# Plain float32 matmuls in three of the four transform stages of a Fourier mixing and feed-forward kernel

## The chip, the cores and the metric

The kernel runs on one core of a Trainium2 chip, as one launch. The metric is the time on the device in microseconds (us); a smaller time is better. TensorE (PE, with its weight loads shown apart as PEld), VectorE (DVE), ScalarE (ACT), GpSimd (POOL) and the DMA queues of SyncE (SP) and POOL take part.

## The reference, cut to what matters

The input `x` has 4 batches of 3072 rows and 256 columns, all float32. Three layers follow one another; the change touches the first alone, the Fourier mixing.

```python
X = np.fft.rfft(x, axis=1)                      # along the 3072 rows
Xr, Xi = X.real.astype(np.float32), X.imag.astype(np.float32)
Yr = Xr @ w_r - Xi @ w_i + b_r
Yi = Xr @ w_i + Xi @ w_r + b_i
Yr = np.sign(Yr) * np.maximum(np.abs(Yr) - lam, 0.0)      # lam = 0.01, Yi likewise
y = np.fft.irfft(Y, n=3072, axis=1)             # Y = Yr + 1j*Yi
# then: a token-shifted feed-forward layer (256 -> 1024 -> 256, squared relu, sigmoid gate)
# then: a second feed-forward layer (256 -> 2048 -> 256, h * clip(h + 3, 0, 6) / 6)
```

## The kernel before, in words

A transform of 3072 rows is made as 96 x 32 with two matmul stages in each direction. Per batch there are four transform stages and the mixing between them:

- `s1` multiplies a 96 x 96 table `f1` with the rows of `x`. A chunk is 96 partitions x 512 elements; each batch has 16 chunks, two to a step. The result goes through ACT to DRAM (`sc_a`).
- `mid` walks over 12 blocks `j`. It reads a chunk of 128 x 512 from `sc_a`. `s2(j)` multiplies each of the chunk's four 128 x 128 pieces, as the stationary operand, with a table of 192 columns (`tt`). Block 0 has a piece of three tables of 64, 64 and 128 columns, twice, with the extra table `tex`. `mix(j)` is the product with `w_r` and `w_i`, followed by the soft threshold; `ia(j)` is the first inverse stage. The result goes to `sc_b`.
- `ib` is the last inverse stage. A chunk of 96 x 512 from `sc_b` is four stationary pieces of 96 x 128, against the 96 x 96 table `fi`. Two chunks make one step, and a batch has 8 steps. The result goes to `sc_y`, from where the first feed-forward layer (`u_r`, `u_k`, `u_v`) reads it.

Matmuls run in the type F32R, whose operands the kernel rounds to 12 significant bits (`_round12`, line 36, for the tables). For float32 accuracy each operand is divided into a rounded part and the remainder (`split`, lines 152 to 155: ACT writes the high part, DVE the low part), and `three` (line 157) adds three products: high by high, low by high, high by low. The tables come divided from the host. `ib` instead lays the high and the low table side by side as one moving operand of 192 columns, multiplies it with the high and the low data (lines 450 and 451), and adds the two halves of the result afterwards (ACT line 454, DVE line 455).

Chunks are loaded by `load_chunks` (line 266, SP queue, 5 buffers `a`), divided by `split_chunks` (line 277, 4 buffers each of `ah` and `al`) and used by `take`. `fetch` (line 296) divides up to four chunks past those in use and loads four more than that. All transform stages share the chunk list, in program order.

PE, ACT, DVE and POOL run in the order in which the program is written; SP's order is planned. PSUM tiles of two banks come from a ring of three (`ptile`, line 149), shared by the transforms and the first feed-forward layer. `first` (line 481) holds the transforms of batch 0 and part of batch 1, which run before the feed-forward layer starts; the remaining transform steps (`later`) are drawn one by one between the units of the first feed-forward layer. The weights of the feed-forward layers arrive as 64-bit floats and are decoded on ACT and DVE (lines 203 to 219) beside this. The second feed-forward layer (lines 739 to 841) comes last and has no transforms beside it.

Of the kernel before, what the change touches and what calls it, by code (L numbers as in the profile page):

```python
# [9 lines left out]
F32 = mybir.dt.float32  # L10
# [15 lines left out]
LAM = 0.01  # L26

# [20 lines left out]
def _tables():  # L48
# [45 lines left out]
    ext = np.stack(_pair(fwd[0, :, 0, 64:128]), 1)  # L94
    fwd = np.concatenate([fwd[:, :, :, 0:64], fwd[:, :, :, 128:256]], 3)
    tab = np.zeros((NP + 2, 128, 2, 640), np.float32)
    tab[:NP, :, :, 0:384] = np.concatenate(_pair(fwd), 3)
    tab[2:, :, :, 384:640] = np.concatenate(_pair(inv), 3)
    small = np.concatenate([*_pair(f1), *_pair(f1.T)], 1)
# [4 lines left out]
def fourier_mix_ffn_kernel(  # L104
# [133 lines left out]
    with tc.manual_schedule(engines=order):  # L238
# [4 lines left out]
        f1 = cst.tile([N1, 2, N1], F32R, name="f1")  # L243
        pad(cst, 128)
        fi = cst.tile([N1, 2, N1], F32R, name="fi")
# [8 lines left out]
        tex = fp.tile([128, 2, 64], F32R, name="tex")  # L254
# [6 lines left out]
        head = {"load": 0, "split": 0, "use": 0}  # L261
# [4 lines left out]
        def load_chunks(upto):  # L266
            while head["load"] < min(len(chunks), upto) and chunks[head["load"]][1] in ready:
                n = head["load"]
                src, _, p = chunks[n]
                if pad_a:  # L270
                    pad(fp, pad_a.pop())
                a = fp.tile([128, 2, D], F32, tag="a", bufs=5, name="a")
                nc.sync.dma_start(out=a[:p], in_=src)
                live[n] = (a[:p], p)
# [12 lines left out]
        def take(n):  # L287

            u = head["use"]
            load_chunks(u + n)  # L290
            split_chunks(u + n)
            r = [live.pop(u + i) for i in range(n)]
            head["use"] = u + n
            return r

        def fetch():

            split_chunks(head["use"] + 4)
            load_chunks(head["split"] + 4)

        def s1(b, lo, hi):
            for s in range(lo, hi):
                p = ptile("s1")
# [12 lines left out]
                yield  # L316
# [16 lines left out]
        def mid(b):  # L333
# [6 lines left out]
            def s2(j):  # L340
                ((h, l),) = take(1)
                t = tt[b, j]
                p = ptile("s2")
                for g in range(2):
                    for dt in range(2):
                        d = slice(128 * dt, 128 * dt + 128)
                        hl = (h[:, g, d], l[:, g, d])
                        if j or g:
                            c = 512 * g + 192 * dt
# [45 lines left out]
            def ia(j):  # L395
                yh, yl = yy.pop(j)
                t = tt.pop((b, j + 2))[:, :, 384:640]
# [40 lines left out]
        def ib(b, lo, hi):  # L438
            ty = sc_y[b].rearrange("a p n -> p a n")
            r = fi.rearrange("p s n -> p (s n)")  # L440
            for c in CHUNKS[lo:hi]:
                n0 = N1 + 4 * c * N1
                sb = fp.tile([128, 2, 4, N1], F32, tag="ev", bufs=3, name="ysb")
                for q, (h, l) in enumerate(take(2)):
                    p = ptile("ib").rearrange("p (a n f) -> p a n f", a=2, n=2)
                    for et in range(2):
                        e = slice(128 * et, 128 * et + 128)
                        for i in range(2):
                            o = p[:, et, i, 0:192]
                            nc.tensor.matmul(o, h[:, i, e], r, start=True, stop=False)  # L450
                            nc.tensor.matmul(o, l[:, i, e], r, start=False, stop=True)  # L451
                    co = fp.tile([128, 512], F32, tag="co", bufs=2, name="co")
                    co = co[:, 0:384].rearrange("p (a n f) -> p a n f", a=2, n=2)
                    nc.scalar.activation(co, p[:, :, :, 96:192], AF.Copy)
                    nc.vector.tensor_add(sb[:, :, 2 * q : 2 * q + 2], p[:, :, :, 0:96], co)
# [11 lines left out]
        def plan(kind, b, lo=0, hi=0):  # L467
            if kind == "s1":
                v = x[b].rearrange("(p n) d -> p n d", n=N2)
                chunks.extend((v[:, 2 * c : 2 * c + 2], None, N1) for c in range(2 * lo, 2 * hi))  # L470
                return kind, s1(b, lo, hi)
            if kind == "mid":
                v = sc_a[b].rearrange("(j g c) n d -> j (c n) g d", g=2, c=4)
                chunks.extend((v[j], ("a", b), 128) for j in range(NP))
                return kind, mid(b)
            for c in CHUNKS[lo:hi]:
                chunks.extend((sc_b[b][:, n : n + 2], ("b", b), N1) for n in (4 * c, 4 * c + 2))
# [17 lines left out]
        nc.gpsimd.dma_start(out=f1.rearrange("p s n -> p (s n)"), in_=small[:, 0 : 2 * N1])  # L495
        load_chunks(5)
# [356 lines left out]
        split_chunks(4)  # L853
        load_chunks(7)
# [18 lines left out]
        for step, _ in enumerate(stream(first)):  # L873
# [8 lines left out]
            if step == LOAD_FI:  # L882
                nc.gpsimd.dma_start(out=fi.rearrange("p s n -> p (s n)"), in_=small[:, 2 * N1 : 4 * N1])
# [194 lines left out]
```

## Time and profile before

| what | value |
|---|---|
| median of 3 runs | 2042.8 us |
| the three runs | 2042.8, 2043.0, 2040.19 us |
| span of the profiled execution | 2040.3 us |
| PE busy | 1978.7 us (97%) |
| PE weight loads busy | 1837.8 us (90%) |
| DVE busy | 1539.0 us (75%) |
| ACT busy | 1330.0 us (65%) |
| mean granted TensorE clock | 0.982 |

The profile gives one time of the profiled execution, its span from the first to the last instruction: 2040.3 us, 2.5 us under the median of the runs. Times inside the trace count from the span's start. A matmul's end is modelled, so the distance between two starts tells more than a duration does. A weight load overlaps the matmul before it. The granted clock is a share of full speed, with the levels 0.5 (1.2 GHz) and 1 (2.4 GHz). A "wait" is idle time of an engine ahead of an instruction, with what ended it.

### The profile page before, as it was taken

The page shows a single profiled execution, that of the slowest core. Times are in us where ns is not written, and L with a number is a line of the kernel's source. Part 1 is how long each engine was busy: PE and PEld are TensorE (multiplying, and loading weights), DVE is VectorE, ACT ScalarE, POOL GpSimd, SP SyncE. Part 2 cuts the span into 40 slices and gives each one's busy share as a digit, 9 for nine tenths or more (in the row PEclk, how much of TensorE's full clock was granted, in tenths as well). Part 3 has the DMA queues.
Part 4 walks back from the last instruction along what each step waited for, and adds up shares of the span by engine and source line. Part 5 has one row for each costly group of instructions (what it writes and reads, how often), then busy time and mean ns, then how long its engine had stood idle before and what let it go on. Part 6 is the DMA issues. An engine that isn't in the chain of part 4 may idle for free.

```text
span 2040.3 us, 34155 instructions
## 1 busy us (share of the span) xinstructions
PE 1978.7 (97%) x13928; PEld 1837.8 (90%) x13928; DVE 1539.0 (75%) x1929; ACT 1330.0 (65%) x1965; POOL 34.7 (2%) x63
## 2 busy tenths in 40 slices
PE   5879999999999999999999999999999999999998
PEld 3868998899789988877789999999999999999998
DVE  3768667766776687888878787778877787778876
ACT  4567557655765575666647676666666676666665
POOL 0000000000000000000000000000000000000000
PEclk7978999999999999999999999999999999999999
DMA  9776447544653352222110110010100110000100
GB/s 255 229 220 188 123 117 217 184 134 124 209 172 112 93 173 89 83 68 85 54 31 22 32 32 22 22 28 26 32 22 22 32 32 22 22 27 27 32 11 22
DMA packets 106991, 175.88 MB, mean 86 GB/s; under 512 B 12945, under 2 KB 63314, under 8 KB 106834
## 3 DMA queue, kind: packets, MB, share of 16 engines
q1 hardware_dynamic: 96034, 141.76, 22.4%
q0 software_dynamic: 10480, 31.67, 5.8%
q8 instruction: 109, 1.79, 0.4%
q14 instruction: 48, 0.39, 0.1%
q10 hardware_dynamic: 320, 0.26, 0.0%
HBM read 110.35 MB, written 63.31 MB: 85 GB/s over the span
## 4 chain that ended last, share of the span: by engine, by line
PE 80%; DVE 11%; ACT 5%; DMA 3%; issue 2%; SPq 0%; ACTq 0%; DVEq 0%
PE oacc L835 25%; PE rq L835 15%; PE acc L163 9%; PE pk L163 8%; PE cc L835 6%; PE mix L163 6%; PE s L163 4%; PE pr L163 2%; DVE g L585 2%; DVE gl L586 1%; PE ia L163 1%; PE ib L450 1%; PE ib L451 1%; PE pi L163 1%; DVE xf L543 1%
## 5 line engine op out<-in xcount | busy, mean ns | idle before, releaser
L835 PE MATMUL oacc<-wo_hi,gl 128*128 128x256 f32 x1536 | 425.6, 277 | 1.1 <-DVE gl L776 1.1
L835 PE MATMUL oacc<-wo_hi,gh 128*128 128x256 f32 x1536 | 426.2, 277 | 0.0
L835 PE MATMUL oacc<-wo_lo,gh 128*128 128x256 f32 x1536 | 424.7, 276 | 0.0
L835 PEld LDWEIGHTS oacc<-wo_hi,gl 128*128 128x128 f32 x1536 | 289.2, 188 | 1.8 <-DVE gl L776 1.5
L835 PEld LDWEIGHTS oacc<-wo_hi,gh 128*128 128x128 f32 x1536 | 289.1, 188 | 0.2
L835 PEld LDWEIGHTS oacc<-wo_lo,gh 128*128 128x128 f32 x1536 | 288.6, 188 | 0.0
L767 DVE SCALAR_TENSOR_TENSOR g<-g,c 128x1024 f32<-128x1024 f32 x184 | 225.5, 1226 | 53.0 <-ACT g L763 52.5
L776 DVE TENSOR_TENSOR gl<-g,gh 128x1024 fp32r<-128x1024 f32 x184 | 225.3, 1224 | 49.8 <-ACT gh L773 46.9
L763 ACT ACTIVATE g<-c,half 128x1024 f32<-128x1024 f32 x184 | 211.8, 1151 | 5.1 <-DVE c L758 4.9
L753 ACT ACTIVATE s<-rq 128x256 f32<-128x256 f32 x184 | 70.5, 383 | 220.9 <-PE rq L835 220.9
L835 PE MATMUL rq<-th,sw 128*128 128x256 f32 x1104 | 212.0, 281 | 0.1
L757 DVE TENSOR_TENSOR c<-rq,s 128x512 f32<-128x512 f32 x184 | 126.8, 689 | 97.2 <-ACT s L753 97.1
L773 ACT ACTIVATE gh<-g 128x1024 fp32r<-128x1024 f32 x184 | 193.7, 1053 | 1.6 <-DVE g L767 1.6
L585 DVE TENSOR_TENSOR g<-g 128x1024 f32<-128x1024 f32 x96 | 117.4, 1223 | 79.6 <-ACT gh L584 79.4
L835 PEld LDWEIGHTS rq<-th,sw 128*128 128x128 f32 x1104 | 168.8, 189 | 0.3 <-ACT s L742 0.3
L163 PE MATMUL acc<-gl,wv_hi 128*128 128x512 f32 x384 | 151.8, 395 | 7.1 <-DVE gl L586 6.9
L835 PE MATMUL rq<-tl,sw 128*128 128x256 f32 x552 | 155.0, 281 | 0.6 <-DVE tl L716 0.6
L163 PE MATMUL pk<-kh,wk_hi 128*128 128x512 f32 x384 | 150.6, 392 | 0.8 <-ACT g L580 0.8
L163 PE MATMUL acc<-gh,wv_hi 128*128 128x512 f32 x384 | 151.3, 394 | 0.0
L163 PE MATMUL acc<-gh,wv_lo 128*128 128x512 f32 x384 | 150.2, 391 | 0.0
L163 PE MATMUL pk<-kl,wk_hi 128*128 128x512 f32 x384 | 149.7, 390 | 0.0
L163 PE MATMUL pk<-kh,wk_lo 128*128 128x512 f32 x384 | 149.5, 389 | 0.0
(152 smaller groups left out, 4955.7 us busy)
## 6 DMA issues: line engine op xcount, KB each, us to landing
tt<-in_tab_dram POOLq DMA_DIRECT2D x40, 640.0 KB, 4.8
yt<-sc_y SPq DMA_DIRECT2D x23, 608.0 KB, 3.9
a<-in_x_dram SPq DMA_DIRECT2D x64, 192.0 KB, 3.7
sc_a<-s1sb SPq DMA_DIRECT2D x32, 384.0 KB, 3.9
a<-sc_a SPq DMA_DIRECT2D x48, 256.0 KB, 3.4
sc_b<-iasb SPq DMA_DIRECT2D x48, 256.0 KB, 4.3
a<-sc_b SPq DMA_DIRECT2D x64, 192.0 KB, 3.1
sc_y<-ysb SPq DMA_DIRECT2D x32, 384.0 KB, 2.8
```

Of the source, the lines that this page charges most:

```text
L163: nc.tensor.matmul(o, a, c, start=first and i == 0, stop=last and i == n - 1, **kw)
L450: nc.tensor.matmul(o, h[:, i, e], r, start=True, stop=False)
L451: nc.tensor.matmul(o, l[:, i, e], r, start=False, stop=True)
L543: nc.vector.scalar_tensor_tensor(o, y[:, a, 0 : hi - lo], mus[:, w, a : a + 1], o, op0=ALU.mult, op1=ALU.add)
L585: nc.vector.tensor_mul(g, g, g)
L753: nc.scalar.activation(s[:, 3], q, AF.Copy)
L757: nc.vector.tensor_add(c[:, 1::2], two(rq), s[:, 0:2])
L763: nc.scalar.activation(g, c, AF.Relu, bias=half, scale=1.0 / 6.0)
L767: nc.vector.scalar_tensor_tensor(g, g, 1.0, tmp["c"], op0=ALU.min, op1=ALU.mult)
L773: nc.scalar.activation(h, tmp["g"], AF.Copy)
L776: nc.vector.tensor_sub(hg[i, j][1], tmp["g"], hg[i, j][0].bitcast(F32))
L835: return lambda: nc.tensor.matmul(o, lhs, rhs, start=start, stop=stop, skip_group_check=True)
```

## The change

`s1`, `s2` and `ib` take the loaded chunk as it is, with undivided float32 tables, one plain float32 matmul in place of three (or, in `ib`, two) F32R matmuls. The chunks' division (`split_chunks`, the tiles `ah` and `al`) goes. `ib` puts both chunks of a step into one PSUM tile, one bank each, and copies the result out by ACT for one half of the columns and by DVE for the other, with no sum. Loads run up to `AHEAD` = 8 chunks past those in use, with 10 buffers; the first call loads 8 chunks instead of 5. The tables shrink: 448 columns per block instead of 640, and half of `f1`, `fi` and `tex`. `mix` and `ia` stay as they are.

```diff
-        f1 = cst.tile([N1, 2, N1], F32R, name="f1")
+        f1 = cst.tile([N1, N1], F32, name="f1")
-        fi = cst.tile([N1, 2, N1], F32R, name="fi")
+        fi = cst.tile([N1, N1], F32, name="fi")
-        tex = fp.tile([128, 2, 64], F32R, name="tex")
+        tex = fp.tile([128, 64], F32, name="tex")
@@ load_chunks
-                a = fp.tile([128, 2, D], F32, tag="a", bufs=5, name="a")
+                a = fp.tile([128, 2, D], F32, tag="a", bufs=AHEAD + 2, name="a")
-        def split_chunks(upto):
-            while head["split"] < min(upto, head["load"]):
-                n = head["split"]
-                a, p = live[n]
-                h = fp.tile([128, 2, D], F32R, tag="ah", bufs=4, name="ah")
-                l = fp.tile([128, 2, D], F32R, tag="al", bufs=4, name="al")
-                split(a, h[:p], l[:p])
-                live[n] = (h[:p], l[:p])
-                head["split"] += 1
@@ fetch
-            split_chunks(head["use"] + 4)
-            load_chunks(head["split"] + 4)
+            load_chunks(head["use"] + AHEAD)
@@ s1
-                for i, (h, l) in enumerate(take(2)):
-                    three(p[:N1, 512 * i : 512 * i + 512], [((f1[:, 0], f1[:, 1]), (flat(h), flat(l)))])
+                for i, a in enumerate(take(2)):
+                    nc.tensor.matmul(p[:N1, 512 * i : 512 * i + 512], f1, flat(a), start=True, stop=True)
@@ load_t
-                t = fp.tile([128, 2, 640], F32R, tag="t", bufs=3, name="tt")
-                c = slice(0 if j < NP else 384, 640 if j >= 2 else 384)
+                t = fp.tile([128, 2, 448], F32R, tag="t", bufs=3, name="tt")
+                c = slice(0 if j < NP else 192, 448 if j >= 2 else 192)
@@ s2
-                            three(p[:, c : c + 192], [(hl, (t[:, g, 0:192], t[:, g, 192:384]))])
+                            mm(512 * g + 192 * dt, 192, a[:, g, d], t[:, g, 0:192])
                         else:
-                            three(p[:, c : c + 64], [(hl, (t[:, g, 0:64], t[:, g, 192:256]))])
-                            three(p[:, c + 64 : c + 128], [(hl, (tex[:, 0], tex[:, 1]))])
-                            three(p[:, c + 128 : c + 256], [(hl, (t[:, g, 64:192], t[:, g, 256:384]))])
+                            mm(c, 64, a[:, g, d], t[:, g, 0:64])
+                            mm(c + 64, 64, a[:, g, d], tex)
+                            mm(c + 128, 128, a[:, g, d], t[:, g, 64:192])
@@ ib
-                for q, (h, l) in enumerate(take(2)):
-                    p = ptile("ib").rearrange("p (a n f) -> p a n f", a=2, n=2)
+                p = ptile("ib").rearrange("p (q f) -> p q f", q=2)[:, :, 0 : 4 * N1]
+                p = p.rearrange("p q (a n f) -> p q a n f", a=2, n=2)
+                for q, a in enumerate(take(2)):
                     for et in range(2):
                         for i in range(2):
-                            nc.tensor.matmul(o, h[:, i, e], r, start=True, stop=False)
-                            nc.tensor.matmul(o, l[:, i, e], r, start=False, stop=True)
-                    nc.scalar.activation(co, p[:, :, :, 96:192], AF.Copy)
-                    nc.vector.tensor_add(sb[:, :, 2 * q : 2 * q + 2], p[:, :, :, 0:96], co)
+                            lhs = a[:, i, 128 * et : 128 * et + 128]
+                            nc.tensor.matmul(p[:, q, et, i], lhs, fi, start=True, stop=True)
+                for et in range(2):
+                    o = sb[:, et].rearrange("p (q n) f -> p q (n f)", q=2)
+                    v = p[:, :, et].rearrange("p q n f -> p q (n f)")
+                    if et:
+                        nc.vector.tensor_copy(o, v)
+                    else:
+                        nc.scalar.activation(o, v, AF.Copy)
@@ before the loops
-        load_chunks(5)
+        load_chunks(AHEAD)
```

## Rows read from the trace of the kernel before

**Rows 1.** The page's first part: busy time, share of the span, instructions.

```profile
PE 1978.7 (97%) x13928; PEld 1837.8 (90%) x13928; DVE 1539.0 (75%) x1929; ACT 1330.0 (65%) x1965; POOL 34.7 (2%) x63
```

**Rows 2.** Busy us by stretch: length, PE, PEld, DVE, ACT, POOL, clock, DMA, GB/s.

```profile
0.00:42.00 42.00, 22.08 (x61) 12.07 (x61) 13.25 (x25) 21.71 (x32) 3.37 (x9) 0.85 0.90 251
42.00:131.20 89.20, 73.47 (x529) 70.36 (x530) 67.15 (x107) 53.18 (x88) 8.28 (x14) 0.88 0.73 222
131.20:141.50 10.30, 6.18 (x18) 3.35 (x16) 2.56 (x4) 5.82 (x10) 0.54 (x1) 0.68 0.84 263
141.50:200.40 58.90, 53.90 (x256) 47.30 (x257) 50.16 (x80) 45.84 (x76) 1.07 (x2) 0.74 0.64 198
200.40:816.00 615.60, 612.28 (x3616) 538.64 (x3616) 434.15 (x553) 387.95 (x548) 21.47 (x37) 1.00 0.48 146
...
1071.00:2040.30 969.30, 963.00 (x8296) 962.20 (x8294) 761.47 (x900) 661.61 (x1033) 0.00 (x0) 1.00 0.09 26
```

**Rows 3.** Groups by line and form: busy us, mean ns, idle before, releasers.

```profile
L155 DVE TENSOR_TENSOR al<-a,ah 96x512 fp32r<-96x512 f32 x128 | 82.8, 682 | 45.5 <-ACT ah L154 45.5
L154 ACT ACTIVATE ah<-a 96x512 fp32r<-96x512 f32 x128 | 74.3, 622 | 15.3 <-DMA a<-in_x_dram 9.5 <-DMA a<-sc_b 5.6
L455 DVE TENSOR_TENSOR ysb<-ib,co 128x384 f32<-128x384 f32 x64 | 33.5, 551 | 13.5 <-ACT co L454 13.4
L155 DVE TENSOR_TENSOR al<-a,ah 128x512 fp32r<-128x512 f32 x48 | 31.7, 683 | 0.8 <-ACT ah L154 0.8
```

**Rows 4.** PE's timeline in `s1`, start and duration in us: low, then full clock.

```profile
8.45 1.06 PE L163 MATMUL s<-ah,f 96*96 96x512 f32 x2
...
9.73 1.06 PE L163 MATMUL s<-ah,f 96*96 96x512 f32 x2
...
22.57 0.62 PE L163 MATMUL s<-ah,f 96*96 96x512 f32 x2
...
23.26 0.62 PE L163 MATMUL s<-ah,f 96*96 96x512 f32 x2
```

**Rows 5.** PE's timeline in `s2`: 64 columns at low clock, 192 at full.

```profile
45.51 0.40 PE L163 MATMUL s<-tex,ah 128*128 128x64 f32 x1
45.73 0.40 PE L163 MATMUL s<-tex,al 128*128 128x64 f32 x1
...
62.17 0.39 PE L163 MATMUL s<-tt,ah 128*128 128x192 f32 x2
...
62.50 0.39 PE L163 MATMUL s<-tt,ah 128*128 128x192 f32 x2
```

**Rows 6.** PE's timeline in `ib` at full clock, two pieces' starts.

```profile
378.01 0.28 PE L450 MATMUL ib<-fi,ah 96*128 96x192 f32 x1
...
378.24 0.27 PE L450 MATMUL ib<-fi,ah 96*128 96x192 f32 x1
```

**Rows 7.** PE's waits from 200.4 to 816 us: us in total, times, longest.

```profile
PE ib L450 <- DVE ysb L455: 3.1, 3, 1.8
```

**Rows 8.** PE's waits from 42 to 131.2 us.

```profile
PE mix L163 <- DVE yf L384: 8.7, 5, 2.0
PE s L163 <- ACT ah L154: 8.1, 1, 8.1
PE s L163 <- DVE al L155: 2.7, 1, 2.7
```

**Rows 9.** PE's timeline: two starts after idle time, idle us and releaser.

```profile
16.10 1.17 PE L163 MATMUL s<-ah,f 96*96 96x512 f32 x2 [3.73 <-ACT ah L154]
...
182.97 0.53 PE L450 MATMUL ib<-fi,ah 96*128 96x192 f32 x1 [2.19 <-DVE ysb L455]
```

**Rows 10.** The chain of waits in `mid` of batch 0: start, us, what.

```profile
76.82 4.60 PE mix L163 x24
...
84.31 0.96 DVE Xl L155
...
89.97 4.63 PE mix L163 x24
```

More of the change, by code (lines that the diff above doesn't have):

```diff
@@ L26 @@
 LAM = 0.01
+AHEAD = 8
 CHUNKS = (1, 2, 3, 4, 5, 6, 7, 0)
@@ L93, in _tables @@
     inv = inv.reshape(NP, 2, 128, 128).transpose(0, 2, 1, 3)
-    ext = np.stack(_pair(fwd[0, :, 0, 64:128]), 1)
+    ext = fwd[0, :, 0, 64:128].astype(np.float32)
     fwd = np.concatenate([fwd[:, :, :, 0:64], fwd[:, :, :, 128:256]], 3)
[L96 to L99, printed above, removed]
+    tab = np.zeros((NP + 2, 128, 2, 448), np.float32)
+    tab[:NP, :, :, 0:192] = fwd
+    tab[2:, :, :, 192:448] = np.concatenate(_pair(inv), 3)
+    small = np.concatenate([f1, f1.T], 1).astype(np.float32)
     return [np.ascontiguousarray(a) for a in (tab, ext, small)]
@@ L253, in fourier_mix_ffn_kernel @@
         bias = fp.tile([128, 3, D], F32, name="bias")
-        tex = fp.tile([128, 2, 64], F32R, name="tex")
+        tex = fp.tile([128, 64], F32, name="tex")
         chunks = []
         ready = set()
-        head = {"load": 0, "split": 0, "use": 0}
+        head = {"load": 0, "use": 0}
         live = {}
@@ L268, in load_chunks @@
                 n = head["load"]
-                src, _, p = chunks[n]
+                src, _, p, _ = chunks[n]
                 if pad_a:
                     pad(fp, pad_a.pop())
-                a = fp.tile([128, 2, D], F32, tag="a", bufs=5, name="a")
+                a = fp.tile([128, 2, D], F32, tag="a", bufs=AHEAD + 2, name="a")
                 nc.sync.dma_start(out=a[:p], in_=src)
-                live[n] = (a[:p], p)
+                live[n] = a[:p]
                 head["load"] += 1
-        def split_chunks(upto):
-            while head["split"] < min(upto, head["load"]):
-                n = head["split"]
-                a, p = live[n]
-                h = fp.tile([128, 2, D], F32R, tag="ah", bufs=4, name="ah")
-                l = fp.tile([128, 2, D], F32R, tag="al", bufs=4, name="al")
-                split(a, h[:p], l[:p])
-                live[n] = (h[:p], l[:p])
-                head["split"] += 1
         def take(n):
@@ L290, in take @@
             load_chunks(u + n)
-            split_chunks(u + n)
             r = [live.pop(u + i) for i in range(n)]
@@ L340, in s2 @@
             def s2(j):
-                ((h, l),) = take(1)
-                t = tt[b, j]
+                (a,) = take(1)
+                t = tt[b, j].bitcast(F32)
+                mm = lambda c, w, lhs, rhs: nc.tensor.matmul(p[:, c : c + w], lhs, rhs, start=True, stop=True)
                 p = ptile("s2")
@@ L396, in ia @@
                 yh, yl = yy.pop(j)
-                t = tt.pop((b, j + 2))[:, :, 384:640]
+                t = tt.pop((b, j + 2))[:, :, 192:448]
                 p = ptile("ia")
@@ L439, in ib @@
             ty = sc_y[b].rearrange("a p n -> p a n")
-            r = fi.rearrange("p s n -> p (s n)")
             for c in CHUNKS[lo:hi]:
@@ L443, in ib @@
                 sb = fp.tile([128, 2, 4, N1], F32, tag="ev", bufs=3, name="ysb")
-                for q, (h, l) in enumerate(take(2)):
-                    p = ptile("ib").rearrange("p (a n f) -> p a n f", a=2, n=2)
+                p = ptile("ib").rearrange("p (q f) -> p q f", q=2)[:, :, 0 : 4 * N1]
+                p = p.rearrange("p q (a n f) -> p q a n f", a=2, n=2)
+                for q, a in enumerate(take(2)):
                     for et in range(2):
-                        e = slice(128 * et, 128 * et + 128)
                         for i in range(2):
-                            o = p[:, et, i, 0:192]
-                            nc.tensor.matmul(o, h[:, i, e], r, start=True, stop=False)
-                            nc.tensor.matmul(o, l[:, i, e], r, start=False, stop=True)
-                    co = fp.tile([128, 512], F32, tag="co", bufs=2, name="co")
-                    co = co[:, 0:384].rearrange("p (a n f) -> p a n f", a=2, n=2)
-                    nc.scalar.activation(co, p[:, :, :, 96:192], AF.Copy)
-                    nc.vector.tensor_add(sb[:, :, 2 * q : 2 * q + 2], p[:, :, :, 0:96], co)
+                            lhs = a[:, i, 128 * et : 128 * et + 128]
[7 more added lines that the diff above has]
+                        nc.scalar.activation(o, v, AF.Copy)
                 nc.sync.dma_start(out=ty[:, :, n0 : n0 + 4 * N1], in_=sb.rearrange("p a n f -> p a (n f)"))
@@ L469, in plan @@
                 v = x[b].rearrange("(p n) d -> p n d", n=N2)
-                chunks.extend((v[:, 2 * c : 2 * c + 2], None, N1) for c in range(2 * lo, 2 * hi))
+                chunks.extend((v[:, 2 * c : 2 * c + 2], None, N1, True) for c in range(2 * lo, 2 * hi))
                 return kind, s1(b, lo, hi)
@@ L473, in plan @@
                 v = sc_a[b].rearrange("(j g c) n d -> j (c n) g d", g=2, c=4)
-                chunks.extend((v[j], ("a", b), 128) for j in range(NP))
+                chunks.extend((v[j], ("a", b), 128, False) for j in range(NP))
                 return kind, mid(b)
             for c in CHUNKS[lo:hi]:
-                chunks.extend((sc_b[b][:, n : n + 2], ("b", b), N1) for n in (4 * c, 4 * c + 2))
+                chunks.extend((sc_b[b][:, n : n + 2], ("b", b), N1, False) for n in (4 * c, 4 * c + 2))
             return kind, ib(b, lo, hi)
@@ L493, in fourier_mix_ffn_kernel @@
         wv = Weights(kw_p, w_v, 8, D, "wv")
-        nc.gpsimd.dma_start(out=f1.rearrange("p s n -> p (s n)"), in_=small[:, 0 : 2 * N1])
-        load_chunks(5)
+        nc.gpsimd.dma_start(out=f1, in_=small[:, 0:N1])
+        load_chunks(AHEAD)
         nc.vector.memset(zero, 0.0)
@@ L849, in store @@
                     at += m
-        split_chunks(4)
-        load_chunks(7)
         loads = decoder(wr.jobs + wk.jobs + wv.jobs, stage1)
@@ L882, in fourier_mix_ffn_kernel @@
             if step == LOAD_FI:
-                nc.gpsimd.dma_start(out=fi.rearrange("p s n -> p (s n)"), in_=small[:, 2 * N1 : 4 * N1])
+                nc.gpsimd.dma_start(out=fi, in_=small[:, N1 : 2 * N1])
             if step in DECODE:
```

2 lines of the change are left out of this document (removed).

## The prediction, made before the result was known

> **What bounds the kernel now.** The first view to read is the page's busy line: PE is busy for 97% of the span, DVE for 75%, ACT for 65% [rows 1]. A share of busy time is a mean over unlike stages, so the second view is the table by stretch [rows 2]. From 200.4 to 816 us PE is busy for 612.3 of 615.6 us at the full clock, while DVE is busy for 434 and ACT for 388: there only PE's own time counts, and relief on DVE or ACT is worth little. From 1071 us on there is no transform. The first 200.4 us are another matter: PE is busy for 155.6 of them, and the granted clock has means of 0.85, 0.88, 0.68 and 0.74 in the four stretches. Of its levels, 0.5 and 1 (1.2 and 2.4 GHz), a mean of 0.74 says that the low one held for about half of the time. Here PE waits for others, and what it waits for decides. The third view, the starts on PE's timeline, gives the price of a product [rows 4 to 6]; the fourth, PE's waits and the chain, says who comes last [rows 7 to 10].
>
> **Price of a product.** An F32R product of 512 columns takes 0.23 us at full clock (three from 22.57 to 23.26) and 0.427 us at low clock (three from 8.45 to 9.73) [rows 4]. One of 192 columns takes 0.111 us [rows 5], more than its 192/512 of 0.23, which is 0.086. At low clock one of 64 columns takes 0.22 us, twice 0.111, though it has a third of the columns [rows 5]. So short products pay a floor of 0.11 us at full clock, which is the load of their 128 stationary columns and not the stream.
>
> The trace shows no plain float32 product. The nearest rows bound it. The kernel rounds each F32R operand to 12 significant bits and divides its data for that reason; a product of undivided operands needs all four products of the halves, where the kernel makes three. I take two passes, one for each half of the stationary operand, in each of which both halves of the moving operand stream: two passes of twice the columns, each with one load beside it. Ends of the price: 4 x 0.2133 us (half of the low-clock 0.427, no time lost between products) and, above, a load that nothing hides (rival B).
>
> - `s1`, 1024 columns a pass: 0.853 to 0.92 (4 x 0.23), taken 0.89, where three products take 0.69 [rows 4]: **+0.20 us a chunk**.
> - `s2`, 384 columns: 0.75 x 0.23 = 0.17 a pass, 0.345 for two, where three take 0.333 (62.17 to 62.50 [rows 5]): **+0.012** a piece; the low end is 0.32.
> - `s2`, block 0: nine products, 9 x 0.111 = 1.0, become six passes of 128, 128 and 256 columns, all near the floor: 0.67, so **-0.33** each.
> - `ib`, 192 columns a pass: the same two loads and columns as now, 0.23 a piece [rows 6]: **0**. If a plain load has a lower floor, 2 x 0.086 = 0.172, so -0.058.
>
> **Where only PE counts.** By the code, 34 `s1` chunks are drawn after the first part, and batches 1 to 3 have 138 ordinary `s2` pieces, 6 of block 0 and 192 of `ib`. That is 34 x 0.20 = 6.8, plus 1.7, minus 2.0, plus 0: **+6.5 us**. The divisions leave DVE and ACT: 82.8 and 31.7 us of `al` on DVE, about as much on ACT [rows 3]. `ib`'s sum on DVE (64 x 0.55 us) becomes 32 copies of the same size, half of it [rows 3]. That shortens the only wait of PE in this stretch, 3.1 us for `ysb` [rows 7]; I take back 2.5. Together **+4.0 us**.
>
> **The first 200 us.** Start: PE idles 3.73 us at 16.10 for a division that waits for its chunk [rows 9]. The new first call issues eight chunks, not five, ahead of the two weight loads, and a buffer is free as soon as PE has read it. But DMA is busy for 0.90 of this stretch [rows 2], and `s1` gets dearer. I take **-3**, ends -5 and +6 (rival C). The depth itself is not new: four divided and four more loaded are eight now.
>
> First blocks of `mid`: PE stops 8.1 us until `ah` is there and then 2.7 us for `al`, which on DVE stands behind two small vector instructions that wait for a transfer [rows 8]. Without a division PE starts when the chunk lands: 0.62 (one `ah` [rows 3]) and 2.7 us earlier. Block 0 at the low clock saves two times three floors of 0.22, 1.3 us. Late next is the low half of the mixing weights, behind `Xl` on DVE. Taken **-4**, ends 0 and -5.
>
> Loop of `mid` of batch 0: the chain runs `mix`, `ia`, `s2`, `Xh`, `Xl`, `yl`, a weight decode, `yf`, and `mix` again: 13.15 us for two blocks (76.82 to 89.97 [rows 10]). No `ah` or `al` is on it, and `s2` costs the same: **0**, although DVE is busy for 67 of 89 us [rows 2]. `mix` waits for `yf` 8.7 us in total [rows 8], and that stays. Ends -4 and +4, with the clock at which `mix` falls.
>
> End of that `mid`: two `al` (1.36 us [rows 3]) stand on DVE ahead of the last `yl`, and dearer `s1` steps lie between on PE. **-1**, ends -2 and +1.
>
> `ib` of batch 0, 141.5 to 200.4 us: DVE is busy for 50.2 of 58.9 us and PE's clock is 0.74 [rows 2]. Both chunks of a step now share one PSUM tile, so a step claims one of the ring's three where it claimed two; its copies start only after the second chunk, about 0.9 us later for the first, and the two run side by side. The wait of 2.19 us at 182.97 [rows 9], behind decode and divisions, should go. After it the `ib` products are 0.21 us apart, low clock, so it costs some 3 us more. Taken **-4**, ends 0 and -14, the latter if the clock stays high throughout: half of the 58.9 us at half speed.
>
> **Sum:** +4.0 - 3 - 4 + 0 - 1 - 4 = **-8 us**. The span of 2040.3 becomes 2032.3; the 2.5 us between span and median are carried over: 2042.8 - 8 = **2035**.
>
> SP's queue: a load waited for the `al` that frees its buffer, with stores queued behind it; with ten buffers the slot it needs belongs to a chunk already used. I cost that at nothing beyond the start. The smaller tables save DMA time, which only the start feels.
>
> **Rivals.** *A, the forecast:* 0.62. For it: `al` on DVE where PE waits, and the prices above.
>
> *B, the loads of plain products are not hidden:* 0.13. Each pass then pays its stream and a load of 0.11 in turn. `s1` is 1.12 (+0.43 x 34 = 15), `s2` 0.57 (+0.24 x 138 = 33), `ib` 0.40 (+0.17 x 192 = 33): +81 in place of +6.5, **2110, slower**. Against it: for F32R the load lies beside the stream [rows 4 to 6]. There are some 760 passes after 200 us, so slower by 0.2% begins at 16 ns more a pass.
>
> *C, the clock stays low in the first 200 us:* 0.15. A chunk of `s1` at low clock takes 1.71, not 1.28. Twenty take 34 us; PE's 22.1 busy us there [rows 2] and some 6 idle us between would hold 28. So +6 in place of -3, and the -4 of `ib` is lost as well: **2048**. It decides once more than about 12 of 20 run at low clock. For it: the clock there is 0.85 already, and waits remain.
>
> *D, one pass is enough:* 0.07. Then the columns double but the loads don't: `s1` 0.46 (-0.23 x 34), `s2` 0.17 (-0.16 x 138), `ib` 0.115 (-0.115 x 192), block 0 about as in A: -54 in place of +6.5, **1974**. Against it: four products of halves don't fit in two streams. The Trainium skill, "Perfetto Trace Analysis", section Engine Utilization, puts the output rate of FP32_LOW_HIGH at half; if that is the whole product and not one pass of it, it is D. No row here shows it.
>
> *E, the relief buys nothing* (transfers set the start, chains elsewhere stay), and gains cancel the +4: 0.03, **2042**.
>
> **How the numbers follow.** A is likeliest: 2035. Its own range, with the ends of the prices and of the first 200 us, is 2019 to 2044. B and D (0.20 together) are left out; C is taken in: 2016 to 2050. About 0.2%, 4 us, is what a measurement can tell from no change. Faster: 0.53 of A, 0.02 of C, all of D: 0.62. Same: 0.06 of A, 0.06 of C, E: 0.15. Slower: 0.03 of A, 0.07 of C, B: 0.23.
>
> **What would show it.** On PE's timeline: `s1` products 0.89 us a chunk, `s2` pieces 0.345, `ib` pieces 0.23; over 0.95, 0.40 and 0.30 speak for B, half of them for D. In the table: the steady stretch about 4 us longer, PE still full, DVE at some 340 us in place of 434. The first `mix` some 7 us earlier; two blocks of the loop still 13 us; the `ysb` waits gone. The forecast is wrong if the loop of `mid` gets shorter, which would mean that its chain was not as read, or if the steady stretch gets shorter.

## The result and the profile after

The kernel after takes 2019.9 us (median of 4 runs, 2019.21 to 2020.22), the kernel before 2042.57 (4 runs, 2040.19 to 2043.0): a ratio of 0.9894 [0.9881, 0.9908], 22.7 us faster. The forecast was 2035, so the direction holds and the size is off by a factor of nearly three (8 us forecast, 22.7 measured). The profiled execution has a span of 2018.1 us; its page answers to [rows 1]:

```profile
PE 1970.9 (98%) x13656; PEld 1812.8 (90%) x13656; DVE 1417.5 (70%) x1721; ACT 1228.0 (61%) x1757; POOL 34.6 (2%) x63
```

PE's busy time fell by 7.8 us, a third of the gain; the rest was idle time. The table by stretch over the same times as [rows 2] (columns as there):

```profile
0.00:42.00 42.00, 27.85 (x66) 13.42 (x66) 2.64 (x10) 14.38 (x15) 4.47 (x11) 0.88 0.93 263
42.00:131.20 89.20, 71.47 (x459) 61.38 (x459) 57.38 (x90) 45.55 (x71) 7.63 (x13) 0.92 0.68 210
...
141.50:200.40 58.90, 58.64 (x334) 52.68 (x333) 39.05 (x53) 37.55 (x51) 1.60 (x3) 0.93 0.59 185
200.40:816.00 615.60, 615.21 (x3412) 530.56 (x3412) 362.68 (x423) 325.88 (x418) 20.94 (x36) 1.00 0.45 134
```

Equal times hold unequal work here, because the kernel after is ahead. So the starts of the same instruction in both traces say where the gain arose (timelines of ACT, DVE and PE; us from the span's start):

| start of | before | after | difference |
|---|---|---|---|
| the eighth copy out of `s1` (batch 0 done) | 29.77 | 24.19 | -5.6 |
| first `yf` of `mid` | 55.89 | 50.79 | -5.1 |
| fourth `yf` | 76.08 | 71.08 | -5.0 |
| last `yf` of batch 0 | 123.83 | 115.23 | -8.6 |
| first `ib` product | 142.13 | 132.00 | -10.1 |
| second sigmoid (`r`) of the feed-forward layer | 205.97 | 186.45 | -19.5 |
| 17th sigmoid (transforms done) | 818.15 | 795.69 | -22.5 |
| end | 2040.32 | 2018.06 | -22.3 |

Start and first blocks gave 5.1 us (forecast 7), the loop of `mid` 3.5 (0), its end 1.5 (1), `ib` of batch 0 9.4 (4), and the steady stretch 2.9, where 4.0 were to be lost.

PE's waits in the first 210 us answer to [rows 8] and [rows 9]. The waits for `ah` and `al` are gone; in the transforms' products loads stand in their place. The largest wait is another: `ia` stands 7.1 us for `yh`, 5.8 of it once, behind the late first `yf` (e8). The loads:

```profile
PE s L332 <- DMA a<-sc_a: 5.7, 1, 5.7
...
PE ib L437 <- DMA a<-sc_b: 3.0, 1, 3.0
PE s L295 <- DMA a<-in_x_dram: 2.5, 4, 1.1
```

PE's timeline after shows the prices (start, duration, instruction). A plain product has two MATMUL rows, so `x4` in `s1` is two chunks, `x8` in `s2` four pieces, `x16` in `ib` eight:

```profile
205.43 1.46 PE L332 MATMUL s<-tt,a 128*128 128x192 f32 x8
206.59 0.53 PE L164 MATMUL pk<-kh,wk_hi 128*128 128x512 f32 x1
206.96 0.40 PE L164 MATMUL pk<-kh,wk_lo 128*128 128x512 f32 x1
...
293.80 1.88 PE L295 MATMUL s<-a,f 96*96 96x512 f32 x4
...
295.75 0.28 PE L164 MATMUL ia<-yl,tt 128*128 128x256 f32 x1
...
358.06 1.92 PE L437 MATMUL ib<-fi,a 96*128 96x96 f32 x16
359.77 0.47 PE L164 MATMUL pr<-kh,wr_hi 128*128 128x512 f32 x1
360.08 0.39 PE L164 MATMUL pr<-kh,wr_lo 128*128 128x512 f32 x1
```

The instruction right behind a plain product is recorded too early, so I count to the one after it and take off the products between. `s2`: 206.96 - 205.43 - 0.23 = 1.30, or 0.325 a piece. `s1`: 295.75 - 293.80 less two `ia` products of 0.113 is 1.72, or 0.86 a chunk. `ib`: 360.08 - 358.06 - 0.23 = 1.79, or 0.224 a piece.

The chain of waits after, two blocks of the loop (start, us, what), answers to [rows 10]:

```profile
83.30 0.61 DVE yf L372
...
85.14 0.71 ACT Xh L155
85.87 0.96 DVE Xl L156
...
87.48 0.74 PE ia L164 x4
88.22 1.31 PE s L332 x8
...
95.42 0.61 DVE yf L372
```

It is 12.12 us from `yf` to `yf` (83.30 to 95.42) in place of 13.15, and `mix` is not on the chain any more.

### The profile page after: what moved, and what is told of

Same layout as the page of the kernel before. It is cut to its first block, busy times and chain, and to the rows that moved or that the text cites. A ratio compares the mean times of both kernels' runs of the same rounds, so it can differ in the third digit from the quotient of the medians.

```text
span 2018.1 us, 33029 instructions
## 1 busy us (share of the span) xinstructions
PE 1970.9 (98%) x13656; PEld 1812.8 (90%) x13656; DVE 1417.5 (70%) x1721; ACT 1228.0 (61%) x1757; POOL 34.6 (2%) x63
## 4 chain that ended last, share of the span: by engine, by line
PE 81%; DVE 11%; ACT 5%; DMA 2%; issue 1%; ACTq 0%; SPq 0%; DVEq 0%; POOLq 0%
PE oacc L824 25%; PE rq L824 16%; PE acc L164 9%; PE pk L164 8%; PE cc L824 6%; PE mix L164 5%; PE ib L437 3%; PE s L332 3%; PE pr L164 2%; PE s L295 2%; DVE g L574 2%; DVE gl L575 2%; PE ia L164 1%; PE pi L164 1%; ACT gh L573 1%
## 5 line engine op out<-in xcount | busy, mean ns | idle before, releaser
L164 PE MATMUL acc<-gh,wv_hi 128*128 128x512 f32 x384 | 155.6, 405 | 0.0
L164 PE MATMUL pk<-kh,wk_hi 128*128 128x512 f32 x384 | 155.1, 404 | 0.0
```

The source lines that it names most:

```text
L164: nc.tensor.matmul(o, a, c, start=first and i == 0, stop=last and i == n - 1, **kw)
```

## The experiments

Four theories give the letters in the expectations. R: ACT and DVE were relieved of work. P: the plain product itself is what pays. L: the deeper loading pays. Q (formed after the first four): the link pays, that is, PE's product no longer stands behind an instruction of ACT's and DVE's queues. Times are medians; "before" is the kernel before on the same chip. The kernel after was not timed again in these sessions: its own before took 2042.57 us, theirs 2040.5 to 2041.2. A difference "to the kernel after" by medians can therefore be off by some 2 us, and where it is small the starts in the traces decide.

| kernel | us (range, runs) | ratio to before |
|---|---|---|
| e1_tiny_division | 2033.9 (2029.5 to 2037.7, 8) | 0.9962 [0.9951, 0.9973] |
| e2_division_kept | 2027.3 (2023.4 to 2029.0, 3) | 0.9930 [0.9908, 0.9953] |
| e3_five_loads | 2026.5 (2025.0 to 2027.3, 3) | 0.9929 [0.9907, 0.9952] |
| e4_s1_divided | 2025.5 (2024.8 to 2026.2, 2) | 0.9926 [0.9897, 0.9955] |
| e5_s2_divided | 2032.2 (2030.4 to 2034.3, 5) | 0.9957 [0.9944, 0.9970] |
| e6_ib_divided | 2028.7 (2027.9 to 2029.5, 2) | 0.9941 [0.9921, 0.9961] |
| e7_late_s1_divided | 2016.0 (2015.4 to 2016.5, 4) | 0.9879 [0.9863, 0.9896] |
| e8_decode_later | 2016.1 (2014.5 to 2018.0, 4) | 0.9880 [0.9865, 0.9895] |
| e9_both | 2011.2 (2008.5 to 2016.5, 4) | 0.9859 [0.9842, 0.9875] |
| e10_pad | 2013.0 (2012.3 to 2014.9, 4) | 0.9863 [0.9847, 0.9880] |
| e11_both_pad | 2005.4 (2002.7 to 2007.0, 4) | 0.9826 [0.9811, 0.9840] |
| e12_filler | 2019.4 (2016.3 to 2023.8, 4) | 0.9895 [0.9872, 0.9918] |

### e1: the kernel before with next to no division work

```diff
-                h = fp.tile([128, 2, D], F32R, tag="ah", bufs=4, name="ah")
-                l = fp.tile([128, 2, D], F32R, tag="al", bufs=4, name="al")
-                split(a, h[:p], l[:p])
+                h, l = pairs[n % 4]          # four tiles, filled once
+                split(a[:, :, 0:1], h[:p, :, 0:1], l[:p, :, 0:1])
```

> The kernel before, its three F32R products and its order unchanged, but each chunk's division writes one element in 256 into four fixed pairs of tiles that were filled once; the products then run on the filled tiles, so the division's work on ACT and DVE is left out and its place in the order kept. Theory R (relief: the gain of the first 200 us comes from ACT and DVE, which divide no more): most of the 22 us comes without any plain product, the second sigmoid product some 15 to 20 us earlier than before, 2020 to 2028 us in all. Theory P (product: plain products, with longer passes, keep PE busy and its clock up): only the waits for ah and al go, 2036 to 2042 us.

2033.9 us against 2040.9, 7.0 faster: between the ranges of R and P. PE's waits in the first 210 us hardly changed:

```profile
PE s L163 <- ACT ah L154: 12.5, 6, 6.1
...
PE ib L456 <- ACT ah L154: 2.8, 1, 2.8
PE s L163 <- DVE al L155: 2.5, 1, 2.5
```

`ah` and `al` take 0.2 us now, yet PE waits 12.5 and 2.5 us for them. Most of the 12.5 is the load behind `ah`, since the loads keep their depth of before: the longest wait, 6.1 us, ends 0.3 us after the chunk has landed. The 2.5 for `al` are DVE's queue. In the steady stretch, from the second to the 17th sigmoid, this kernel gains 2.6 us with the same products; the waits for `ysb` [rows 7] are down to 0.9 us there. The products of this kernel run on constant data, and its granted clock in the first 42 us is 0.76 where it was 0.85; whether the two belong together was not tested.

### e2: the kernel after with the division still done, its results unread

```diff
+                    h = fp.tile([128, 2, D], F32R, tag="ah", bufs=3, name="ah")
+                    l = fp.tile([128, 2, D], F32R, tag="al", bufs=3, name="al")
+                    split(a, h[:p], l[:p])
```

> The changed kernel, with every chunk still divided on ACT and DVE into tiles that nobody reads (three buffers each, up to three chunks past those in use). R: the relief is gone and with it most of the gain, 2034 to 2044 us. P: the products are plain, so the gain stays, 2019 to 2025 us.

2027.3 us, 13.6 under before: between the ranges of P and R. The profiled execution, the fastest of the three, has a span of 2021.7, 18.7 under. In that execution PE waits for no `ah` or `al` at all; ahead of the transforms' products only loads are left:

```profile
PE s L346 <- DMA a<-sc_a: 5.1, 1, 5.1
...
PE s L309 <- DMA a<-in_x_dram: 2.0, 3, 0.8
```

So with the work kept, 13.6 of 22.7 us remain by the medians. Relief of work alone is not the cause; at most the other 9.1 us, two fifths of the gain, need it. This kernel also has the deep loads; e3 tells the two apart.

### e3: the kernel after with five loads and five buffers

```diff
-AHEAD = 8
+AHEAD = 3
-        load_chunks(AHEAD)
+        load_chunks(5)
```

> The changed kernel with five buffers for loaded chunks, five loads in the first call and three past those in use. Theory L (the deeper loading makes the start): the 5.5 us by which the first batch's s1 ends earlier go, 2024 to 2028 us. R and P: the start gains because nothing stands between a chunk's arrival and its product, within 2 us of the changed kernel's 2020.

2026.5, 6.6 over the kernel after by the medians, 5.1 by the spans. PE's waits show it at the start:

```profile
PE s L295 <- DMA a<-in_x_dram: 14.2, 5, 4.8
```

That is 14.2 us in place of 2.5. `s1` of batch 0 ends at 29.57 us, the 5.6 us gained there are gone, and most of them return by the first `yf` (51.72, 0.9 later than after). So the total falls in theory L's range, but not by way of the start: the last `yf` is 0.6 us later than in the kernel after, the first `ib` product 2.2 and the second sigmoid 5.4. `ib` of batch 0 takes 57.6 us at a mean clock of 0.81 in place of 54.5 at 0.84, with 1.9 us of idle PE in place of 0.3. Whether the fewer loads bring that lower clock was not shown.

The first three kernels form a ladder, each against the same before: the work gone, 7.0 us (e1); the work and the link gone, 14.4 (e3); with the deep loads too, 22.7 (the kernel after, against its own runs of before). That gives R 7, Q 7 and L 7 to 8. The step called Q also holds the plain products' price, which nets to about nothing (below), the smaller tables, and `ib`'s shared PSUM tile and copies without a sum, which no run separates. In the profiled executions e3 is 10.2 us ahead of e1: 2.6 by the first `yf`, 2.3 from the loop of `mid`, where the clock is 1.00 in place of 0.93, and 5.2 from `ib` of batch 0, where it is 0.81 in place of 0.76. So part of what is called Q is the clock. e2 is the check: link and loads without the work should give 14 to 16, and gave 13.6. The intervals of e2 and e3 are 4.6 us wide on either side, so the thirds are rough.

### e4 to e6: one stage divided again

In `e4` all of `s1`, in `e5` `s2`, in `e6` `ib` work on divided data as before, three chunks ahead; the other stages stay as in the kernel after. `e5` also has six loads ahead and eight buffers in place of eight and ten. The core of `e4`:

```diff
+                    if isinstance(a, tuple):
+                        three(p[:N1, 512 * i : 512 * i + 512], [((fd[:, 0], fd[:, 1]), (flat(a[0]), flat(a[1])))])
+                    else:
+                        nc.tensor.matmul(p[:N1, 512 * i : 512 * i + 512], f1, flat(a), start=True, stop=True)
```

> The changed kernel with s1 alone put back to divided data and three F32R products (three buffers each for the halves); s2 and ib stay plain. By the trace of after an s1 chunk takes 0.86 us plain and took 0.69 divided: the 34 chunks drawn beside the feed-forward layer give back 5.8 us. R: the first 200 us lose some 4 us at the start, 2016 to 2022 us in all. P: s1's long passes are what keeps the clock up in the first 200 us, 2024 to 2032 us.

2025.5: in theory P's range, later than R's. The link returns at one place. The timelines of DVE and PE (idle time and its releaser in brackets):

```profile
45.68 0.17 DVE L519 TENSOR_SCALAR omu<-mus 128x4 f32<-128x4 f32 x1 [10.33 <-DMA mus<-in_moe_mu_r_dram]
46.80 0.56 DVE L520 TENSOR_SCALAR bias<-bias 128x768 f32<-128x768 f32 x1 [0.95 <-DMA bias<-in_b_r_dram]
47.28 0.68 DVE L156 TENSOR_TENSOR al<-a,ah 96x512 fp32r<-96x512 f32 x1
...
48.01 0.74 PE L164 MATMUL s<-al,fd 96*96 96x512 f32 x1 [9.54 <-DVE al L156]
```

An `al` of 0.68 us stands behind two small vector instructions that wait for transfers, and PE loses 9.5 us: Q in four lines. But `s1` of batch 0 had ended late already, at 32.49 us in place of 24.19, and that is mostly the clock: from 7.07 to 37.30 us the products of a chunk start 0.43 us apart, the low level's spacing [rows 4].

```profile
31.83 0.63 PE L164 MATMUL s<-al,fd 96*96 96x512 f32 x1
32.26 1.05 PE L164 MATMUL s<-ah,fd 96*96 96x512 f32 x2
```

(The view by stretch gives a clock of 1.00 for the first 42 us of this run, which this spacing contradicts; go by the spacing.) In the kernel after the ten chunks from 5.11 us take 11.29 us, 1.13 each, where the low level would make it 1.71. So e4 doesn't tell Q from P: whether the missing link or the longer plain products keep the clock up at the start is open. In the steady stretch the same kernel is 3.9 us shorter than the kernel after (605.38 against 609.24), so the plain `s1` costs there.

> The changed kernel with s2 alone put back to divided chunks, tables and three F32R products (three buffers each for the halves, eight for chunks, six loads ahead). Theory Q, formed after the first four runs (the link: what costs is not the division's work but that PE's product stands behind ACT's and DVE's queues): mid of batch 0 begins some 3 to 5 us later, the rest stays, 2022 to 2027 us. Theory R (the work itself on ACT and DVE): under 1 us lost, 2019 to 2021 us. Beside the feed-forward layer s2 is 1 to 3 us dearer in all by either.

2032.2, later than Q's range; the fewer loads are part of it (`s1` of batch 0 ends 4.9 us later than after). The waits return where [rows 8] had them, the loop is as long as before, and the steady stretch is 2.1 us longer than after's:

```profile
PE s L164 <- ACT ah L155: 5.4, 1, 5.4
...
PE s L164 <- DVE al L156: 3.6, 1, 3.6
```

> The changed kernel with ib alone put back to divided chunks, the 192-column table, two products a piece and the sum on DVE. Q: from the first ib product of batch 0 to the second sigmoid the changed kernel takes 54 us and before took 64; 5 to 9 us of this come back, and the waits for ysb later, 3 us, 2025 to 2032 us. R: the work of 16 divisions alone, with PE's clock as in the changed kernel, 2020 to 2024 us.

2028.7, in Q's range. Its first `ib` product starts 1.5 us later than in the kernel after; `ib` of batch 0 then takes 64.0 us to the second sigmoid, as before (63.8), in place of 54.5:

```profile
PE ib L452 <- ACT ah L155: 3.3, 1, 3.3
PE ib L453 <- DVE al L156: 3.1, 4, 2.0
PE ib L452 <- DVE ysb L457: 2.3, 2, 2.2
```

When the last layer begins it is 16.8 us behind, but at the end only 9.7: the last layer, which no edit touches, is 7 us shorter. e10 follows that up.

### e7: `s1` divided in the 34 late chunks alone

```diff
+                chunks.extend((v[:, 2 * c : 2 * c + 2], None, N1, b > 1 or lo >= FILL[1]) for c in range(2 * lo, 2 * hi))
```

> The changed kernel with only those 34 chunks of s1 divided that are drawn beside the feed-forward layer, where PE alone sets the time and DVE is busy for 363 of 616 us. If the price read from the traces holds there (0.69 us divided, 0.86 plain a chunk), 34 x 0.17 = 5.8 us are gained, 2013 to 2016 us; if the link costs PE as much as in the first 200 us, nothing is gained, 2019 to 2024 us.

2016.0, 3.9 under the kernel after. All of it arises in the steady stretch: PE's busy time there is 604.34 us in place of 608.85, 4.5 less, and 0.7 us of waits for `al` come back. The term has the right sign at four fifths of its size: 4.5 for the 32 of the 34 chunks that lie in this stretch is 0.14 a chunk, where the prices gave 0.17.

### e8: two weight decodes put off until after the first blocks

```diff
-DECODE = tuple(range(9, 13)) + tuple(range(13, 39, 2))
+DECODE = (9, 10) + tuple(range(13, 43, 2))
```

> The changed kernel with the decoding of the first feed-forward weights begun two steps later (the first load stays, each further step follows two steps later), so that DVE doesn't stand before yf of block 0 until the first weight has arrived, 7.1 us in the trace of after. If that wait alone holds up the first block of mid, yf comes 5 to 7 us earlier and the kernel ends at 2013 to 2016 us; if the loop of mid or the weights' own due time take the gain back, 2018 to 2021 us.

2016.1, at the edge of the first range. In the kernel after the first `mix` starts 12.1 us earlier than before, but the first `yf` only 5.1. DVE's timeline of the kernel after:

```profile
42.38 0.95 DVE L156 TENSOR_TENSOR Xl<-s,Xh 128x768 fp32r<-128x768 f32 x1
50.45 0.43 DVE L204 TENSOR_SCALAR stt<-stw 128x512 uint32<-128x512 uint32 x1 [7.11 <-DMA stw<-in_moe_w_r_dram]
50.79 0.68 DVE L372 TENSOR_TENSOR yf<-mix,bias 128x512 f32<-128x512 f32 x1
```

DVE stands 7.11 us for the transfer of a feed-forward weight that is not due for long, with `yf` behind it. With the decode put off:

```profile
42.12 0.95 DVE L156 TENSOR_TENSOR Xl<-s,Xh 128x768 fp32r<-128x768 f32 x1
44.81 0.69 DVE L372 TENSOR_TENSOR yf<-mix,bias 128x512 f32<-128x512 f32 x1 [1.74 <-PE mix L164]
```

The first `yf` is 6.0 us earlier, the last of batch 0 8.9. Of that 3.1 us are left at the second sigmoid and 1.8 at the end: `ib` of batch 0 takes 59.9 us here at a mean clock of 0.77, against 54.5 at 0.84.

### e9: e7 and e8 together

> The late s1 chunks divided and the decoding begun two steps later, together. The first gained 4 us beside the feed-forward layer, the second 4 us at the start: if they add, 2011 to 2014 us; if the decoding's gain hangs on the clock in the ib of batch 0, as in its profile (9 us ahead at the end of mid, 3 at the second sigmoid), 2014 to 2018 us.

2011.2, 8.8 under the kernel after, with runs from 2008.5 to 2016.5: in the range for gains that add, but with a spread that reaches into the other.

### e10 and e11: 384 empty bytes a partition behind `fi`

```diff
         fi = cst.tile([N1, N1], F32, name="fi")
+        pad(cst, 384)
```

> The changed kernel with 384 bytes a partition left empty behind fi, as far as the two-part table of the run with ib divided moved everything placed behind it; no work changes. In that run the second feed-forward layer, whose program is the same, took 967.3 us instead of 974.3 to 974.5. If the place of its tiles is the cause, this kernel takes 7 us less than the changed one, 2011 to 2015 us; if it was something in the divided ib, 2019 to 2021 us.

2013.0, 6.9 under the kernel after by the medians (5.0 by the spans), with the same instructions. The last layer alone, by stretch, in the kernel after:

```profile
1043.58:2018.06 974.48, 967.89 (x8336) 966.90 (x8334) 765.89 (x910) 664.36 (x1037) 0.00 (x0) 1.00 0.09 26
```

and with the empty bytes:

```profile
1045.43:2013.08 967.65, 961.10 (x8336) 960.09 (x8334) 765.74 (x910) 662.45 (x1037) 0.00 (x0) 1.00 0.10 26
```

The same 8336 products take 6.8 us less of PE's time at the full clock. It is the spacing: in the kernel after `cc` products start 0.12 us apart,

```profile
1202.35 0.28 PE L824 MATMUL cc<-xh,wi_lo 128*128 128x256 f32 x1
1202.47 0.28 PE L824 MATMUL cc<-xl,wi_hi 128*128 128x256 f32 x1
```

and with the empty bytes 0.11:

```profile
1203.28 0.28 PE L825 MATMUL cc<-xh,wi_hi 128*128 128x256 f32 x1
1203.39 0.28 PE L825 MATMUL cc<-xh,wi_lo 128*128 128x256 f32 x1
```

Not every product gains so: on the mean over the 8336 it is 0.8 ns each (6.79 us in all). The kernel before has 974.3 us there, so the change itself gained nothing by placement. Why the position matters was not found.

> Late s1 chunks divided, decoding two steps later, and the 384 empty bytes. If the three gains add: 7 us below the run without the empty bytes, 2004 to 2009 us; if the place has no part, 2011 to 2016 us.

2005.4, ratio 0.9826 [0.9811, 0.9840]: e9 with the empty bytes beats both kernels, the one after by 14.5 us. It is in the range for three gains that add.

### e12: products to fill PE's wait ahead of `ib` of batch 0

```diff
+            if b == 0 and lo == 0:
+                p = ptile("fill")
+                for _ in range(3):
+                    nc.tensor.matmul(p[:N1, 0:512], f1, bias[:N1, 0:2].rearrange("p n d -> p (n d)"), start=True, stop=True)
```

> The changed kernel with three plain products of 512 columns, whose result nobody reads, ahead of the first ib product of batch 0; they fill some 2.6 of the 3.0 us in which PE waits there for sc_b. In the trace of after the low clock holds from 133 to 150 us, right behind this wait, and the ib products there take twice as long. If the wait brought the clock down and the low clock sets the length of this stretch, the second sigmoid comes 5 to 8 us earlier and the kernel ends at 2012 to 2015 us. If ACT and DVE set the length, or the clock falls all the same, 2019 to 2022 us.

2019.4, no gain. PE's timeline around the wait:

```profile
128.66 2.74 PE L431 MATMUL fill<-bias,f 96*96 96x512 f32 x6
133.39 5.92 PE L441 MATMUL ib<-fi,a 96*128 96x96 f32 x32 [2.00 <-DMA a<-sc_b]
```

The wait and what follows, by stretch (columns as in [rows 2]):

```profile
131.40:133.39 1.99, 0.00 (x0) 0.03 (x1) 0.00 (x0) 0.26 (x1) 0.00 (x0) 1.00 0.83 242
133.39:152.00 18.61, 18.61 (x75) 15.68 (x76) 7.45 (x14) 8.87 (x16) 0.00 (x0) 0.54 0.88 286
```

The filler keeps PE busy until 131.40; of the wait of 2.98 us, 1.99 are left. The clock still fell, and it fell during the `ib` products, with PE busy for all of the 18.61 us at a mean of 0.54. So filling a third of the wait does not keep the clock up; that the two microseconds left bring it down is not excluded.

## Why the prediction was right and where it was wrong, point by point

**What bounds the kernel.** Right in the main. PE alone counts after 200 us, and in the first 200 it stood behind ACT, DVE and the loads. The ladder divides the gain roughly in three: relief of ACT and DVE; the link, since an instruction in a queue that runs in order waits for the one ahead, however short it is itself (e4, e8), together with what the clock gives; and the loads.

**Price of a product.** As taken. Each product has two MATMUL rows, and at 512 columns each takes 0.43 us of the 0.86, about what twice the columns of an F32R product need (0.46); B (1.12) and D (0.46) fall. The Trainium skill, "FP8 and Floating Point Precision", section TensorE Precision Notes, says that true FP32 goes through the array four times; the trace agrees, with 0.86 us where one F32R product takes 0.23. The Trainium skill, "Perfetto Trace Analysis", section Engine Utilization, puts FP32_LOW_HIGH at half the output rate, which was weighed as D; the trace does not bear that out for the whole product, whose 0.86 us is nearly four times the 0.23. Measured 0.86, 0.325 and 0.224 for the forecast 0.89, 0.345 and 0.23: all three a few per cent too dear.

**Where only PE counts: +4.0 forecast, -2.9 measured.** This step failed by its prices. From the second to the 17th sigmoid PE is busy for 608.86 us of 612.18 before and for 608.85 of 609.24 after: the products net to zero, not +6.5, and the gain is idle time, 3.3 down to 0.4, close to the 2.5 taken. Putting the stages back one at a time shows the terms: `s1` costs 4.5 (e7; 6.8 forecast). `s2` with block 0 saves 2.3 (e5: busy for 611.11; 0.3 forecast). `ib` saves 2 to 4 (e6: 612.79, with up to 1.8 us for 8 more product rows in the stretch; 0 forecast), which its spacing of 0.224 us does not show; where that lies is open. So the terms that were mis-sized are `s1`, too dear, and `s2` and `ib`, too little saved.

**Start: -3 forecast, -5.6 measured** at the end of `s1`. "The depth itself is not new" failed: e3 gives the whole 5.6 back. e3 frees a buffer when PE has read it, as the kernel after does, so it is not the earlier release but the number: eight loads in the first call and ten buffers, where there were five of each. The depth does not do it alone either: e4 has it, and ends `s1` at 32.49 us.

**First blocks: -4 forecast, +0.5 measured** (-5.6 to -5.1). PE's part came and more, 12.1 us at the first `mix`. "Late next is the low half of the mixing weights" named the wrong instruction: it was a weight decode ahead of `yf`, with 7.11 us of idle DVE (e8). The two steps of the first 56 us together were -7 forecast, -5.1 measured.

**Loop of `mid`: 0 forecast, -3.5 measured.** The forecast named this as the sign that the chain was misread, and it was. It has `mix` at 4.6 us [rows 10]; that is `mix` mostly at the low clock (a mean of 0.63 from 76.82 to 81.42 us), and at the full clock its 24 products take 2.8. The step priced the instructions and not the clock at which they ran, although it kept "the clock at which `mix` falls" in its ends. The same stretch, from the fourth to the last `yf`, in the kernel after is

```profile
71.08:115.23 44.15, 37.23 (x283) 35.52 (x284) 32.08 (x50) 26.16 (x43) 4.25 (x7) 1.00 0.61 188
```

and in `e2`, by the same view,

```profile
68.98:115.65 46.67, 39.68 (x283) 38.37 (x284) 37.02 (x59) 29.76 (x50) 4.42 (x7) 0.93 0.59 180
```

and over the kernels its length goes with the granted clock (the seventh column):

| clock | kernels | us |
|---|---|---|
| 0.89 | before; e5 | 47.75; 47.45 |
| 0.93 | e1; e2 | 46.40; 46.67 |
| 0.96 | e7; e8 | 45.19; 45.18 |
| 1.00 | after; e3; e6; e9; e10; e12 | 44.15; 44.14; 44.12; 44.13; 44.11; 44.15 |
| 1.00 | e4 | 44.76 |

e7 and e8 have the same products in this stretch as the kernel after (x283), and with the clock at 0.96 they lose 1.04 us; e2 has 5 us more of DVE work than the kernel after, and e1 with 33.00 us of it is as long. So the length goes with the clock. Why the clock stays high in it is not shown; the absent division alone is not the reason, since e7 and e8 have none there and fall to 0.96.

**End of `mid`: -1 forecast, -1.5 measured.** As taken.

**`ib` of batch 0: -4 forecast, -9.4 measured.** The largest miss. From the first `ib` product to the second sigmoid the view by stretch of the kernel before reads

```profile
142.13:205.97 63.84, 59.47 (x292) 52.40 (x293) 55.30 (x85) 46.94 (x77) 1.07 (x2) 0.76 0.62 193
```

and that of the kernel after

```profile
132.00:186.45 54.45, 54.19 (x286) 47.43 (x287) 33.59 (x47) 31.21 (x46) 1.07 (x2) 0.84 0.73 236
```

Idle time falls from 4.4 to 0.3 us, 4.1 together: about the -4 that the forecast took for it. The rest is the clock: 0.76 of 63.84 us is 30.6 us at the low level, 0.84 of 54.45 is 17.4, and half of the difference is 6.6 us. The two make 10.7 where 9.4 shows; dearer `s1` chunks of batch 1 lie in the stretch and may be the rest. The end of -14 was worked out for just this clock, and the value taken gave it no weight. e6 puts back the division, the sum on DVE and a PSUM tile for each chunk at once, and brings both back (6.2 idle, 0.79, 64.0 us); which of the three does it was not separated.

**Range and rivals.** That the range of 2016 to 2050 held the time is in part luck. Both things that the forecast named as signs of being wrong appeared: the loop of `mid` got shorter, and so did the steady stretch. Start (-5.6, end -5) and first blocks (+0.5, ends 0 and -5) lie just outside their ends. Against the values taken, the steps gave -6.9 (steady), -2.6, +4.5 (first blocks), -3.5, -0.5 and -5.4 us: the first blocks' miss hid a part of the others, and the values taken sat too near to zero wherever the clock entered. C did not come: the first ten chunks take 1.13 us each (5.11 to 16.40 us), not 1.71, and over the span the clock is 0.990 where it was 0.982.

**What stays open.** What makes the clock fall and rise in the first 200 us (e12 only weakens one candidate); whether the link or the longer plain products keep it up at the start (e4); which part of the new `ib` brings its gain (e6); and the spread of e1, e9 and e12, whose single runs differ by some 8 us with the same code. That the clock makes this spread is argued only.

## What to carry to other kernels

A product that costs PE a quarter more (`s1`: 0.86 us for 0.69) can still pay, if it takes two engines out of the path from load to product: use the plain form where ACT and DVE come last, and the divided one where PE alone is the bound and the plain one is dearer (e7). `s2` and `ib`, whose plain products cost no more, gain there too (e5, e6). Look at what stands ahead in an in-order queue, not at how long an instruction takes itself (e4, e8). And price each step of a chain at the clock at which its row was taken, with a second price at the other level.

## What the runs showed of the hardware

- **Position in the on-chip memory moves PE's spacing.** 384 empty bytes a partition ahead of the tiles shorten 8336 products from 967.89 to 961.10 us at an unchanged clock (e10; 960.99 in e11). In e4, e7 and e9, whose table `fd` moves the tiles by 768 bytes, the last layer keeps the longer time.
- **The clock is low under a busy PE.** In the kernel after, behind a wait of 2.98 us that ends at 132.0, the granted clock is 0.99 for 1 us and 0.50 for the next 17, with PE busy for all of them:

```profile
132.00:133.00 1.00, 1.00 (x9) 1.00 (x10) 0.00 (x0) 0.00 (x0) 0.00 (x0) 0.99 0.85 205
133.00:150.00 17.00, 17.00 (x66) 14.39 (x66) 6.75 (x14) 8.18 (x16) 0.00 (x0) 0.50 0.90 292
```

- **The row behind a plain product starts too early.** In the kernel after the gap to the next row shows it: 206.59 to 206.96 is 0.37 us, where that product takes 0.23.
